# The load of w2 split into 11 rows on every partition and 8 rows on 48 partitions, in a decode kernel on one core

## Chip, cores, metric

The kernel runs on one core of a Trainium2 chip. The metric is the device time of one launch in microseconds, the median of three runs.

## The reference

A single decode step for a batch of two: a layer norm, attention of 16 query heads over a window of 2,048 positions of a cache with 8 key/value heads, and a gate from a small two-layer net.

```python
x = A_x                                   # [2, 1, 448], bf16
xn = layernorm(x)
q = xn @ wq                               # 16 heads of 256
p = softmax(q @ k[last 2048].T / 16)      # 8 kv heads, each used by two query heads
s = (p @ v[last 2048]) @ wo               # wo: [4096, 448]
h = maximum(xn @ w1, 0)                   # w1: [448, 1792]
g = silu(h @ w2)                          # w2: [1792, 448]
out = x + s * g
```

K and V of the window are 16.8 MB each, wq and wo 3.7 MB each, w1 and w2 1.6 MB each.

## The kernel before

The kernel writes its instruction lists by hand. `pr.op` and `pr.dma` append one instruction to an engine's list, with the instructions it depends on; `run` turns these into semaphores. Each engine executes its list in order, and so does SP, which issues all large loads: wq, w1, w2, the four loads of K (`d_k`, one for each unit u of 4 heads of one batch row), then V of each unit when that unit's scores are done with the buffer (`load_v`, V of unit 3 in two halves), and at the end wo in five parts of 20, 4, 5, 2 and 1 rows per partition (`WO_PARTS`). ACT issues the three small loads of x and half of the output.

The computation goes in this order. DVE and PE make the layer norm and lay it out as `xr`; PE computes q. `do_H` multiplies `xr` with w1 into the bank `qbk`, in four column groups of the PE array (`tile_position`), 448 columns in each; DVE applies the maximum (`h_n`) and transposes 32 x 32 blocks (`h_sb`), so that row 14p + j of h stands on partition p in block j. `do_F` multiplies these with w2, which is loaded the same way (partition p holds rows 14p to 14p + 13), and DVE and ACT make the gate `g_sb`.

Then DVE transposes K of each unit in place (`do_turn`, 4 instructions a unit), PE computes scores (`do_S`), DVE and ACT the softmax (`do_max`, `do_et`). After the last unit, `do_spread` and `do_pt` lay the probabilities out, `do_PV` multiplies them with V, `do_out` scales, and `do_turn_out` transposes the result into `at2`. The last product, with wo, runs in two stages: 24 rows per partition go to the bank `wbk` in four column groups, are copied to `wc` and added with 8 fp32 matmuls into `fbk`; the last 8 rows go to `fbk` directly, each matmul waiting for its part of wo. Two DVE instructions and two small stores end the kernel.

`fill(n)` issues n fp32 matmuls into a free bank whose result nobody reads. There are 7 fills: one after PV of unit 0, three in the middle of PV of unit 3, one after it, two ahead of the product with wo. PE's code is cut into bodies at marks ("block1" and so on), which are visited or hinted at ahead of their use.

Of the kernel before, what the change touches and what calls it, by code (L numbers as in the profile page):

```python
# [133 lines left out]
def bass_recurrent_scan__sliding_block_cached__dense_activation_relu__decode_kernel(  # L134
# [11 lines left out]
    B, Sq, D = A_x.shape  # L146
# [3 lines left out]
    DFF = B_w1.shape[1]  # L150
# [6 lines left out]
    NU = 4  # L157
    SLOTS = 7
    HC = HD // 2
    FC = DFF // 2  # L160
# [2 lines left out]
    PADW = 5  # L163
    WO_PARTS = [20, 4, 5, 2, 1]
    WO_TILED = 24

    es = contextlib.ExitStack()
    with es:
        pr = _Prog(nc, es)

        def named(name, shape, dt):
            return es.enter_context(nc.sbuf_tensor(name, shape, dt))
# [13 lines left out]
        wqo = named("wqo", [128, 32 * D], BF)  # L186
        assert SLOTS * HC <= 32 * D
        w1_sb = named("w1_sb", [128, SLOTS * FC], BF)
        w2_sb = named("w2_sb", [128, 14 * D], BF)
        ident = named("ident", [128, 128], BF)  # L190
        perm = named("perm", [128, 128], BF)
        par2 = named("par2", [128, 2], F32)
# [14 lines left out]
        xr = named("xr", [128, SLOTS * 4], BF)  # L207
        q_x = named("q_x", [128, 2048], BF)
        qstat = named("qstat", [128, 4 * 256], BF)
        h_n = named("h_n", [128, 448], BF)  # L210
        h_sb = named("h_sb", [128, 448], BF)
        zc = named("zc", [128, D], F32)
        wc = named("wc", [128, D], F32)
        fpad = named("fpad", [128, PADW], F32)
        ea = named("ea", [128, NCOL], F32)
        g_sb = named("g_sb", [128, NCOL], F32)
# [9 lines left out]
        half2 = named("half2", [128, 2], F32)  # L226
        rs = named("rs", [128, 2 * NU], F32)
        pt = [named(f"pt{i}", [128, 512], BF) for i in range(NU)]
        o_odd = named("o_odd", [128, DH], F32)
        at2 = named("at2", [128, 32 * PADW], BF)  # L230

# [17 lines left out]
        d_xc = [pr.dma(ACTE, x_c[32 * h:32 * h + 4, :], half(A_x, h), [p_xc]) for h in range(2)]  # L249
        wq_src = A_wq.rearrange("r (hf c) -> (r hf) c", hf=2).rearrange("(p s) c -> p (s c)", s=SLOTS)  # L250
        w1_src = B_w1.rearrange("r (hf c) -> (r hf) c", hf=2).rearrange("(p s) c -> p (s c)", s=SLOTS)
        w2_src = B_w2.rearrange("(p j) n -> p (j n)", j=14)
        wo_src = A_wo.rearrange("(p j) n -> p (j n)", j=32)

        d_k, d_v, last_S, last_PV = {}, {}, {}, {}
        st = {}
        d_wq = pr.dma(SP, wqo[:, 0:SLOTS * HC], wq_src)
        st["w1"] = pr.dma(SP, w1_sb[:, :], w1_src)
        st["w2"] = pr.dma(SP, w2_sb[:, :], w2_src)
        for u in range(NU):  # L260
            d_k[u] = pr.dma(SP, kv[u][:, :], kv_src(u, A_k_cache))

# [2 lines left out]
            out=ident[:, :], in_=ident[:, :], compare_op=ALU.not_equal, fill=1.0,  # L265
# [7 lines left out]
            out=sd[0:B, 0:1], in0=st2[0:B, 1:2], scalar1=EPS, scalar2=None, op0=ALU.add), [v_ag])  # L273
# [5 lines left out]
        def z(t):  # L279
            return a_z[t.name]  # L280
# [21 lines left out]
        for e2 in range(2):  # L302
            v_xn = pr.op(DVE, lambda e, e2=e2: e.tensor_scalar(
                out=view(xg, 128 - 127 * e2, [[256, 4], [128, 2], [2, 64]], n=B),
                in0=view(x_sb, 3 * e2, [[1, 4], [0, 2], [SLOTS, 64]], n=B),
                scalar1=st2[0:B, 0:1], scalar2=rstd[0:B, 0:1],
                op0=ALU.subtract, op1=ALU.mult), [v_rs])

        def mm(out_ap, lhsT, rhs, start, stop=False, **kw):
            return lambda e: e.matmul(out_ap, lhsT=lhsT, rhs=rhs, start=start, stop=stop,  # L310
                                      skip_group_check=True, **kw)

        for s in range(SLOTS):
# [3 lines left out]
            out=view(xr, 0, [[4, SLOTS], [2, 2], [1, 2]]), in0=view(mbk, 0, [[2, SLOTS], [0, 2], [1, 2]]),  # L317
# [3 lines left out]
        deps = [d_wq, v_xr, z(qbk)]  # L321
        for s in range(SLOTS):
            for i in range(4):
                lo = s * HC + i * 512
                m_q = pr.op(PE, mm(qbk[32 * i:32 * i + 4, :], xr[:, 4 * s:4 * s + 4], wqo[:, lo:lo + 512],
                                   s == 0, s == SLOTS - 1, tile_position=(0, 32 * i)), deps)
                deps = []
        v_q = pr.op(DVE, lambda e: e.tensor_scalar(  # L328
            out=view(q_x, 0, [[256, 8], [128, 2], [1, 32]]), in0=view(qbk, 0, [[64, 8], [1, 2], [2, 32]]),
            scalar1=SCALE, scalar2=None, op0=ALU.mult), [m_q])  # L330
        v_qx = pr.op(DVE, lambda e: e.tensor_copy(
            view(q_x, 32, [[128, 16], [32, 3], [1, 32]]), view(q_x, 0, [[128, 16], [0, 3], [1, 32]])), [v_q])
# [68 lines left out]
        def fill(n):  # L401
            for _ in range(n):
                pr.op(PE, mm(sbk[0][0:8, :], f8[:, :], kv[0][:, 0:1024].bitcast(F32), True, True),
                      [st["exp", 2], d_v[0], v_f8])

        def do_PV(u):
            bank, p, v = obk, pt[u], kv[u]
            deps = [d_v[u], st["pt", u], z(bank), st.get(("osb", u - 1))]
            for n in range(NT // 2):
                i = n % 4  # L410
                if u == NU - 1 and n == NT // 4:
                    fill(3)
                    deps = [d_vb]
                o = pr.op(PE, mm(bank[32 * i:32 * i + 16, :], p[:, 16 * n:16 * n + 16],
                                 v[:, 2 * n * DH:2 * n * DH + 2 * DH],
                                 n < 4, n >= NT // 2 - 4, tile_position=(0, 32 * i)), deps)
                deps = []
            last_PV[u] = o
# [11 lines left out]
        def do_turn_out(hg):  # L430
            deps = [st["osb", 2 + hg], v_as, st["mbk"]]
            lo = 64 * hg
            for dq in range(8):
# [4 lines left out]
            st["at"] = st["mbk"] = pr.op(DVE, lambda e: e.tensor_copy(  # L438
                view(at2, 1, [[2, B], [PADW, 32]], n=64, p0=lo), view(mbk, 288, [[32, B], [1, 32]], n=64, p0=lo)), [o, p_z])

        def do_H():
            deps = [st["w1"], v_xr, v_q]
            for s in range(SLOTS):
                for k in range(4):
                    hf, i = divmod(k, 2)
                    lo = s * FC + i * 448
                    o = pr.op(PE, mm(qbk[32 * k:32 * k + B, 0:448], xr[:, 4 * s + 2 * hf:4 * s + 2 * hf + 2],
                                     w1_sb[:, lo:lo + 448], s == 0, s == SLOTS - 1, tile_position=(0, 32 * k)), deps)
                    deps = []
            v = pr.op(DVE, lambda e: e.tensor_scalar(  # L450
                out=h_n[:, :], in0=view(qbk, 0, [[1, 14], [14, 32]]),
                scalar1=0.0, scalar2=None, op0=ALU.max), [o])
            st["h"] = pr.op(DVE, lambda e: e.transpose(h_sb[:, :], h_n[:, :]), [v])

        def do_F():
            deps = [st["w2"], st["h"], z(fbk)]
            for j in range(14):
                i = j % 4
                o = pr.op(PE, mm(fbk[32 * i:32 * i + B, 0:D], h_sb[:, 32 * j:32 * j + 2], w2_sb[:, j * D:j * D + D],
                                 j < 4, j >= 10, tile_position=(0, 32 * i)), deps)  # L460
                deps = []
            v = pr.op(DVE, lambda e: e.tensor_copy(zc[:, :], fbk[:, 0:D]), [o])
            deps = [v, v_fp, st["mbk"]]
            for c in range(4):
                k, h = divmod(c, 2)
                o = pr.op(PE, mm(mbk[32 * h:32 * h + 4, 0:NCOL], fpad[:, 1 - k:5 - k],
                                 zc[:, NCOL * c:NCOL * c + NCOL], k == 0, k == 1, tile_position=(0, 32 * h)), deps)
                deps = []
            a_e = pr.op(ACTE, lambda e: e.activation(ea[0:ROWS, :], mbk[0:ROWS, 0:NCOL], ACT.Exp, scale=-1.0), [o])
            v = pr.op(DVE, lambda e: e.tensor_scalar(  # L470
                out=ea[0:ROWS, :], in0=ea[0:ROWS, :], scalar1=1.0, scalar2=None, op0=ALU.add), [a_e])
            v = pr.op(DVE, lambda e: e.reciprocal(tmp[0:ROWS, :], ea[0:ROWS, :]), [v])
            st["g"] = st["mbk"] = pr.op(DVE, lambda e: e.tensor_tensor(
                out=g_sb[0:ROWS, :], in0=mbk[0:ROWS, 0:NCOL], in1=tmp[0:ROWS, :], op=ALU.mult), [v])
# [30 lines left out]
        for u in range(NU):  # L505
            do_PV(u)
            if u == 0:
                pr.mark("block2")
            if u in (0, NU - 1):
                fill(1)  # L510
            do_out(u)
            if u >= 2:
                do_turn_out(u - 2)
# [13 lines left out]
        v_wc = pr.op(DVE, lambda e: e.tensor_copy(wc[:, :], wbk[:, 0:D]), [o])  # L527
        pr.mark("late")
        deps = [st["g"]]

        for c in range(4):
            k, h = divmod(c, 2)
            pr.op(PE, mm(fbk[32 * h:32 * h + 4, 0:NCOL], fpad[:, 1 - k:5 - k],
                         wc[:, NCOL * c:NCOL * c + NCOL], k == 0, tile_position=(0, 32 * h)), deps + [v_wc])
        for j in range(WO_TILED, 32):
            for c in range(4):
                k, h = divmod(c, 2)
                lo = j * D + c * NCOL
                m_o = pr.op(PE, mm(fbk[32 * h:32 * h + 4, 0:NCOL], at2[:, PADW * j + 1 - k:PADW * j + 5 - k],
                                   wqo[:, lo:lo + NCOL], False, j == 31,  # L540
                                   tile_position=(0, 32 * h)), deps + [landed.get(j)])
                deps = []
# [3 lines left out]
            out=tmp[0:ROWS, :], in0=fbk[0:ROWS, 0:NCOL], in1=g_sb[0:ROWS, :], op=ALU.mult), [m_o, st["g"]])  # L546
# [35 lines left out]
```

## Time and profile before

| | |
|---|---|
| time of the launch, median of 3 | 110.18 us (110.14 to 110.25) |
| profiled execution, first to last instruction | 108.7 us |
| outside the span, by the median | about 1.5 us |
| moved from HBM | 44.11 MB, 406 GB/s over the span |
| PE busy | 58.9 us (54%), 469 matmuls |
| DVE busy | 61.5 us (57%), 84 instructions |
| ACT busy | 9.0 us (8%) |
| queue of the SP and ACT loads (q1), share of 16 engines | 95.2% |

The profile gives no launch time of its own for the profiled execution, so its span of 108.7 us is set beside the median. A core has 16 DMA engines; "DMA share" in the windows is the mean over them of the time in which a packet was under way. Queue q1 carries what SP issues and q10 what ACT issues; q8 carries instruction code. A line such as `17.99 2.78 PE L310 MATMUL qbk<-w_sb,xr ... x28` reads: from 17.99 us, for 2.78 us, 28 matmuls that write qbk. L310 is the line of a helper that all matmuls share, and L39 that of all DMA issues.

### The profile page before, as it was taken

The page shows a single profiled execution, that of the slowest core. Times are in us where ns is not written, and L with a number is a line of the kernel's source. Part 1 is how long each engine was busy: PE and PEld are TensorE (multiplying, and loading weights), DVE is VectorE, ACT ScalarE, POOL GpSimd, SP SyncE. Part 2 cuts the span into 40 slices and gives each one's busy share as a digit, 9 for nine tenths or more (in the row PEclk, how much of TensorE's full clock was granted, in tenths as well). Part 3 has the DMA queues.
Part 4 walks back from the last instruction along what each step waited for, and adds up shares of the span by engine and source line. Part 5 has one row for each costly group of instructions (what it writes and reads, how often), then busy time and mean ns, then how long its engine had stood idle before and what let it go on. Part 6 is the DMA issues. An engine that isn't in the chain of part 4 may idle for free.

```text
span 108.7 us, 1117 instructions
## 1 busy us (share of the span) xinstructions
PE 58.9 (54%) x469; PEld 15.8 (14%) x469; DVE 61.5 (57%) x84; ACT 9.0 (8%) x18; POOL 2.1 (2%) x13
## 2 busy tenths in 40 slices
PE   0001295650000069919961995299438967769672
PEld 0000023120000012101200220011023222303131
DVE  2920007634099979999999999940448332303021
ACT  2970000000000000002000200020020000000000
POOL 7000000000000000000000000000000000000000
PEclk9999999995555557995898599769965699999999
DMA  6899999989988999899989998999899899999960
GB/s 165 338 450 391 414 429 520 395 386 507 458 386 386 483 470 398 386 470 470 410 386 470 470 410 386 458 483 410 386 458 483 356 422 428 434 428 429 391 253 1
DMA packets 2487, 44.16 MB, mean 406 GB/s; under 512 B 306, under 2 KB 564, under 8 KB 820
## 3 DMA queue, kind: packets, MB, share of 16 engines
q1 hardware_dynamic: 2456, 44.11, 95.2%
q8 instruction: 3, 0.05, 0.2%
q10 hardware_dynamic: 28, 0.00, 0.0%
HBM read 44.11 MB, written 0.00 MB: 406 GB/s over the span
## 4 chain that ended last, share of the span: by engine, by line
DMA 55%; DVE 29%; PE 10%; SPq 4%; issue 1%
DMA kv<-in_A_k_cache_dram 32%; DVE kv L345 24%; DMA wqo<-in_A_wo_dram 22%; PE sbk L310 7%; SPq L39 4%; PE fbk L310 1%; PE wbk L310 1%; DVE q_x L374 1%; DVE rm L362 1%; DVE wc L527 1%; DVE rm_t L364 0%; DVE bias L368 0%; DVE bt L365 0%; DVE tmp L545 0%; DVE out_sb L547 0%
## 5 line engine op out<-in xcount | busy, mean ns | idle before, releaser
L310 PE MATMUL sbk<-kv,qstat 128*8 128x512 bf16 x128 | 30.0, 1083 | 23.0 <-DVE kv L345 23.0
L345 DVE STREAM_TRANSPOSE kv<-kv 128x2048 f32<-128x2048 f32 x16 | 35.6, 2274 | 4.6 <-DMA kv<-in_A_k_cache_dram 4.6
L310 PEld LDWEIGHTS sbk<-kv,qstat 128*8 128x8 bf16 x128 | 5.2, 107 | 46.1 <-DVE kv L345 29.0
L310 PE MATMUL obk<-kv,pt 128*16 128x512 bf16 x128 | 9.5, 441 | 2.5 <-DVE xg L426 1.2
L423 DVE TENSOR_SCALAR o_odd<-obk,rs 128x256 f32<-128x256 f32 x4 | 1.9, 484 | 11.0 <-PE obk L310 11.0
L310 PE MATMUL sbk<-kv,f 128*8 128x512 f32 x14 | 7.1, 629 | 0.0
L369 ACT ACTIVATE e_sb<-sbk,bias 128x512 bf16<-128x512 f32 x4 | 2.7, 687 | 51.8 <-DVE bias L368 51.8
L310 PE MATMUL qbk<-wqo,xr 128*4 128x512 bf16 x28 | 3.2, 626 | 4.2 <-DMA wqo<-in_A_wq_dram 4.2
L362 DVE TENSOR_REDUCE rm<-sbk 128x1 f32<-128x512 f32 x4 | 2.6, 661 | 4.8 <-PE sbk L310 4.8
L310 PE MATMUL mbk<-ident,xg 2*128 2x2 bf16 x7 | 0.3, 160 | 8.4 <-issue 8.4
L328 DVE TENSOR_SCALAR q_x<-qbk 128x512 bf16<-128x512 f32 x1 | 0.7, 692 | 7.2 <-PE qbk L310 7.2
L310 PEld LDWEIGHTS obk<-kv,pt 128*16 128x16 bf16 x128 | 3.2, 97 | 8.6 <-issue 5.0
L374 DVE STREAM_TRANSPOSE q_x<-e_sb 128x512 bf16<-128x512 bf16 x4 | 2.8, 691 | 1.7 <-ACT e_sb L369 1.7
L391 DVE TENSOR_TENSOR pt<-spk,pmask 128x512 bf16<-128x512 f32 x4 | 2.6, 683 | 0.8 <-PE spk L310 0.8
L310 PE MATMUL qbk<-w_sb,xr 128*2 128x448 bf16 x28 | 2.8, 572 | 0.0
L527 DVE COPY wc<-wbk 128x448 f32<-128x448 f32 x1 | 0.6, 625 | 3.8 <-PE wbk L310 3.8
L310 PE MATMUL spk<-q_x,perm 128*32 128x128 bf16 x16 | 0.6, 297 | 3.1 <-DVE q_x L374 3.1
L339 DVE CAST qstat<-mbk 32x256 bf16<-32x256 f32 x4 | 1.7, 420 | 0.7 <-PE mbk L310 0.7
L426 DVE SCALAR_TENSOR_TENSOR xg<-obk,rs,o_odd 128x256 bf16<-128x256 f32 x4 | 1.9, 484 | 0.1
L310 PE MATMUL wbk<-wqo,at 128*2 128x448 bf16 x24 | 1.3, 352 | 1.0 <-DMA wqo<-in_A_wo_dram 1.0
L270 DVE BATCH_NORM_STATS2 st<-x_sb 2x6 f32<-2x448 bf16 x1 | 0.6, 615 | 2.1 <-DMA x_sb<-in_A_x_dram 2.1
L310 PEld LDWEIGHTS sbk<-kv,f 128*8 128x8 f32 x14 | 1.3, 96 | 3.1 <-issue 2.6
(72 smaller groups left out, 33.0 us busy)
## 6 DMA issues: line engine op xcount, KB each, us to landing
kv<-in_A_k_cache_dram SPq DMA_DIRECT2D x4, 4096.0 KB, 39.7
kv<-in_A_v_cache_dram SPq DMA_DIRECT2D x3, 4096.0 KB, 22.1
kv<-in_A_v_cache_dram SPq DMA_DIRECT2D x2, 2048.0 KB, 17.6
wqo<-in_A_wq_dram SPq DMA_DIRECT2D x1, 3584.0 KB, 12.1
w_sb<-in_B_w_dram SPq DMA_DIRECT2D x2, 1568.0 KB, 17.0
wqo<-in_A_wo_dram SPq DMA_DIRECT2D x1, 2240.0 KB, 24.4
wqo<-in_A_wo_dram SPq DMA_DIRECT2D x1, 560.0 KB, 25.7
wqo<-in_A_wo_dram SPq DMA_DIRECT2D x1, 448.0 KB, 24.8
```

Of the source, the lines that this page charges most:

```text
L39: o = _Op(eng, lambda e: e.dma_start(dst, src), [d for d in deps if d is not None], True)
L310: return lambda e: e.matmul(out_ap, lhsT=lhsT, rhs=rhs, start=start, stop=stop, skip_group_check=True, **kw)
L328: v_q = pr.op(DVE, lambda e: e.tensor_scalar(out=view(q_x, 0, [[256, 8], [128, 2], [1, 32]]), in0=view(qbk, 0, [[64, 8], [1, 2], [2, 32]]) ...
L339: st["q"] = st["mbk"] = pr.op(DVE, lambda e, Q=Q: e.tensor_copy(qstat[32 * Q:32 * Q + 32, 256 * Q:256 * Q + 256], mbk[32 * Q:32 * Q + 32, ...
L345: st["turn", u] = pr.op(DVE, lambda e, n=n: e.transpose(kf[:, 2048 * n:2048 * n + 2048], kf[:, 2048 * n:2048 * n + 2048]), [d_k[u]])
L362: v = pr.op(DVE, lambda e: e.tensor_reduce(out=rm[:, 0:1], in_=sbk[u % 2][:, :], axis=AX.X, op=ALU.max), [last_S[u], p_z, st.get(("rmt", u ...
L369: st["exp", u] = pr.op(ACTE, lambda e: e.activation(e_sb[:, :], sbk[u % 2][:, :], ACT.Exp, bias=bias[:, 0:1], accum_out=ssum[:, u:u + 1]), ...
L374: st["et", u] = pr.op(DVE, lambda e: e.transpose(q_x[:, 512 * u:512 * u + 512], e_sb[:, :]), [st["exp", u], m_qt])
L391: st["pt", u] = pr.op(DVE, lambda e: e.tensor_tensor(out=view(pt[u], 0, [[8, 64], [2, 4], [1, 2]]), in0=view(spk, 128 * u, [[2, 64], [0, 4 ...
L423: v = pr.op(DVE, lambda e: e.tensor_scalar(out=o_odd[:, :], in0=obk[:, DH:2 * DH], scalar1=rs[:, 2 * u + 1:2 * u + 2], scalar2=None, op0=A ...
L426: st["osb", u] = pr.op(DVE, lambda e: e.scalar_tensor_tensor(out=o_sb[:, lo:lo + DH], in0=obk[:, 0:DH], scalar=rs[:, 2 * u:2 * u + 1], in1 ...
L527: v_wc = pr.op(DVE, lambda e: e.tensor_copy(wc[:, :], wbk[:, 0:D]), [o])
```

## The change

w2 is loaded in two transfers. The first takes rows 0 to 1,407, 11 to a partition. The second takes the last 384 rows, 8 to a partition, to partitions 32 to 79 of a new tile `w2_x`, which DVE zeroes before; its source is walked as twelve blocks, four rows of 7,168 bytes in each. H is cut to match: four column groups of 352 columns in `qbk`, where a group that crosses the middle of w1's columns is two matmuls, and two more matmuls per slot for the last 384 columns into `wbk`. DVE makes the maximum and the transpose for both, and F is 19 matmuls instead of 14. The tiles of h lie in the probabilities' tiles `pt`, `wc` lies in `zc`, and the copy to it also waits for the gate. One fill after PV of unit 0 and one of the three in PV of unit 3 are left out.

```diff
+    W2U = 11
+    W2X = 8
+    XA, XB = 12, 4
+    UC = 32 * W2U
+    UROWS = 128 * W2U
...
-        w2_sb = named("w2_sb", [128, 14 * D], BF)
+        w2_sb = named("w2_sb", [128, W2U * D], BF)
+        w2_x = named("w2_x", [128, W2X * D], BF)
...
-        wc = named("wc", [128, D], F32)
+        wc = zc
...
+        h_n, h_sb, h_nx, h_x = pt
...
-        w2_src = B_w2.rearrange("(p j) n -> p (j n)", j=14)
+        w2_src = B_w2[0:UROWS, :].rearrange("(p j) n -> p (j n)", j=W2U)
+        w2x_src = B_w2[UROWS:DFF, :].rearrange("(b a s) n -> a b (s n)", a=XA, b=XB)
...
         st["w2"] = pr.dma(SP, w2_sb[:, :], w2_src)
+        v_w2x = pr.op(DVE, lambda e: e.memset(w2_x[:, :].bitcast(F32), 0.0))
+        st["w2x"] = pr.dma(SP, w2_x[32:32 + XA * XB, :], w2x_src, [v_w2x])
...
                 if u == NU - 1 and n == NT // 4:
-                    fill(3)
+                    fill(2)
...
+        half_cols = FC
+        pieces = []
+        for k in range(4):
+            lo, at = UC * k, 0
+            while at < UC:
+                hf, c = divmod(lo + at, half_cols)
+                n = min(UC - at, half_cols - c)
+                pieces.append((k, hf, at, c, n))
+                at += n
+
         def do_H():
             deps = [st["w1"], v_xr, v_q]
             for s in range(SLOTS):
-                for k in range(4):
...
+                for k, hf, at, c, n in pieces:
+                    lo = s * FC + c
+                    o = pr.op(PE, mm(qbk[32 * k:32 * k + B, at:at + n], xr[:, 4 * s + 2 * hf:4 * s + 2 * hf + 2],
+                                     w1_sb[:, lo:lo + n], s == 0 and at == 0, s == SLOTS - 1,
+                                     tile_position=(0, 32 * k)), deps)
+                    deps = [z(wbk)] if s == 0 and k == 3 else []
+                for k, na in ((1, 8), (2, XA - 8)):
+                    lo = s * FC + UROWS - half_cols + (k - 1) * 8 * W2X
+                    ox = pr.op(PE, mm(view(wbk, 0, [[64, XB], [1, na * W2X]], n=B, p0=32 * k),
+                                      xr[:, 4 * s + 2:4 * s + 4], view(w1_sb, lo, [[XA * W2X, XB], [1, na * W2X]]),
+                                      s == 0, s == SLOTS - 1, tile_position=(0, 32 * k)), deps)
                     deps = []
...
         def do_F():
-            deps = [st["w2"], st["h"], z(fbk)]
-            for j in range(14):
...
+            deps = [st["w2"], st["w2x"], st["h"], z(fbk)]
+            rows = [(h_sb, w2_sb, j) for j in range(W2U)] + [(h_x, w2_x, j) for j in range(W2X)]
+            for n, (hs, ws, j) in enumerate(rows):
+                i = n % 4
+                o = pr.op(PE, mm(fbk[32 * i:32 * i + B, 0:D], hs[:, 32 * j:32 * j + 2], ws[:, j * D:j * D + D],
+                                 n < 4, n >= len(rows) - 4, tile_position=(0, 32 * i)), deps)
...
-            if u in (0, NU - 1):
+            if u == NU - 1:
                 fill(1)
...
-        v_wc = pr.op(DVE, lambda e: e.tensor_copy(wc[:, :], wbk[:, 0:D]), [o])
+        v_wc = pr.op(DVE, lambda e: e.tensor_copy(wc[:, :], wbk[:, 0:D]), [o, st["g"]])
```

More of the change, by code (lines that the diff above doesn't have):

```diff
@@ L165, in bass_recurrent_scan__sliding_block_cached__dense_activation_relu__decode_kernel @@
     WO_TILED = 24
+    W2U = 11
[3 more added lines that the diff above has]
+    UROWS = 128 * W2U
+    assert UROWS + XA * XB * W2X == DFF
     es = contextlib.ExitStack()
@@ L209, in bass_recurrent_scan__sliding_block_cached__dense_activation_relu__decode_kernel @@
         qstat = named("qstat", [128, 4 * 256], BF)
-        h_n = named("h_n", [128, 448], BF)
-        h_sb = named("h_sb", [128, 448], BF)
         zc = named("zc", [128, D], F32)
-        wc = named("wc", [128, D], F32)
+        wc = zc
         fpad = named("fpad", [128, PADW], F32)
@@ L228, in bass_recurrent_scan__sliding_block_cached__dense_activation_relu__decode_kernel @@
         pt = [named(f"pt{i}", [128, 512], BF) for i in range(NU)]
+        h_n, h_sb, h_nx, h_x = pt
+        assert UC <= 512 and 32 * W2X <= 512
         o_odd = named("o_odd", [128, DH], F32)
@@ L443, in do_H @@
             for s in range(SLOTS):
-                for k in range(4):
[L445 to L448, printed above, removed]
+                for k, hf, at, c, n in pieces:
[4 more added lines that the diff above has]
+                    deps = [z(wbk)] if s == 0 and k == 3 else []
@@ L449, in do_H @@
+                for k, na in ((1, 8), (2, XA - 8)):
[3 more added lines that the diff above has]
+                                      s == 0, s == SLOTS - 1, tile_position=(0, 32 * k)), deps)
                     deps = []
             v = pr.op(DVE, lambda e: e.tensor_scalar(
-                out=h_n[:, :], in0=view(qbk, 0, [[1, 14], [14, 32]]),
@@ L452, in do_H @@
-                scalar1=0.0, scalar2=None, op0=ALU.max), [o])
-            st["h"] = pr.op(DVE, lambda e: e.transpose(h_sb[:, :], h_n[:, :]), [v])
-        def do_F():
-            deps = [st["w2"], st["h"], z(fbk)]
-            for j in range(14):
-                i = j % 4
-                o = pr.op(PE, mm(fbk[32 * i:32 * i + B, 0:D], h_sb[:, 32 * j:32 * j + 2], w2_sb[:, j * D:j * D + D],
-                                 j < 4, j >= 10, tile_position=(0, 32 * i)), deps)
+                out=h_n[:, 0:UC], in0=view(qbk, 0, [[1, W2U], [W2U, 32]]),
@@ new lines, in do_H @@
+                scalar1=0.0, scalar2=None, op0=ALU.max), [ox])
+            vx = pr.op(DVE, lambda e: e.tensor_scalar(
+                out=h_nx[:, 0:32 * W2X], in0=view(wbk, 0, [[1, W2X], [W2X, 8], [64, XB]]),
+                scalar1=0.0, scalar2=None, op0=ALU.max), [ox])
+            st["h"] = pr.op(DVE, lambda e: e.transpose(h_sb[:, 0:UC], h_n[:, 0:UC]), [v])
+            st["h"] = pr.op(DVE, lambda e: e.transpose(h_x[:, 0:32 * W2X], h_nx[:, 0:32 * W2X]), [vx])
+        def do_F():
+            deps = [st["w2"], st["w2x"], st["h"], z(fbk)]
[4 more added lines that the diff above has]
+                                 n < 4, n >= len(rows) - 4, tile_position=(0, 32 * i)), deps)
```

## The prediction

> **What bounds the kernel now.** I read the page first, then the chain of waits, then narrow windows at the end of the span.
>
> ```profile
> DMA  6899999989988999899989998999899899999960
> ...
> DMA packets 2487, 44.16 MB, mean 406 GB/s; under 512 B 306, under 2 KB 564, under 8 KB 820
> ...
> q1 hardware_dynamic: 2456, 44.11, 95.2%
> q8 instruction: 3, 0.05, 0.2%
> q10 hardware_dynamic: 28, 0.00, 0.0%
> ...
> DMA 55%; DVE 29%; PE 10%; SPq 4%; issue 1%
> ```
>
> The DMA engines stand at 8 or 9 tenths from the second slice to the last but two. The chain's DVE 29% has to be looked at, since it could mean that loads wait for VectorE:
>
> ```profile
> 69.88 7.55 PE sbk L310 x21
> ...
> 78.67 24.36 DMA wqo<-in_A_wo_dram
> ...
> 103.16 1.38 PE wbk L310 x24
> ...
> 104.56 0.64 DVE wc L527
> ...
> 105.24 1.42 PE fbk L310 x40
> ```
>
> The first part of wo is issued at 78.67 and lands 24.36 us later. At the mean of 406 GB/s that is 9.9 MB, and V of units 2 and 3 with that part of wo (20 of 32 rows) are 10.7 MB. So when PE at last released these issues, all of V of units 2 and 3 still had to move: the chain through DVE and PE reached the queue about 10 us before the queue needed it. The kernel is one unbroken stream of 44.11 MB; its time is the end of that stream plus the PE and DVE work behind the last landings. How does the stream end?
>
> ```profile
> 104.40:104.60 0.20, 0.11 (x4) 0.00 (x0) 0.04 (x1) 0.00 (x0) 0.00 (x0) 1.00 0.99 363
> 104.60:104.80 0.20, 0.00 (x0) 0.00 (x0) 0.20 (x1) 0.00 (x0) 0.00 (x0) 1.00 0.72 256
> 104.80:105.00 0.20, 0.00 (x0) 0.00 (x0) 0.20 (x1) 0.00 (x0) 0.00 (x0) 1.00 0.45 161
> 105.00:105.20 0.20, 0.00 (x0) 0.00 (x0) 0.18 (x1) 0.00 (x0) 0.00 (x0) 1.00 0.18 63
> 105.20:105.40 0.20, 0.16 (x4) 0.16 (x6) 0.00 (x0) 0.00 (x0) 0.00 (x0) 1.00 0.14 54
> 105.40:105.60 0.20, 0.20 (x8) 0.15 (x6) 0.00 (x0) 0.00 (x0) 0.00 (x0) 1.00 0.44 131
> 105.60:105.80 0.20, 0.20 (x13) 0.20 (x10) 0.00 (x0) 0.00 (x0) 0.00 (x0) 1.00 0.12 40
> 105.80:106.00 0.20, 0.20 (x16) 0.20 (x12) 0.00 (x0) 0.00 (x0) 0.00 (x0) 1.00 0.09 31
> 106.00:106.20 0.20, 0.20 (x16) 0.19 (x12) 0.00 (x0) 0.00 (x0) 0.00 (x0) 1.00 0.02 4
> ```
>
> The last but one column is the mean share of the 16 DMA engines. It falls from 0.99 to 0.18 within 0.6 us, and 0.12 to 0.14 is left until about 106.0: two engines of 16 (2/16 = 0.125) work alone from 105.2 to 106.05. The bump at 105.4 I read as the third packet of the instruction queue (0.05 MB in three packets, 16 KB each). So 14 engines end near 105.2 and two about 0.85 us later. The two other instruction packets belong to the start of the kernel, and two engines are late; 16 KB on one engine are 0.6 us at the rate below, and all later data of that engine stands behind them. I take the lag for theirs.
>
> The landings set the last steps:
>
> ```profile
> 104.14 0.09 PEld L310 LDWEIGHTS wbk<-wqo,at 128*2 128x2 bf16 x4 [0.32 <-DMA wqo<-in_A_wo_dram]
> ```
>
> PE waits for the second part of wo until 104.14; wc, the 8 fp32 matmuls on it and the 32 on the last parts hang on that. A transfer has landed when its last engine is done, so the two late engines set each of these times.
>
> **The change part by part.** The main term is w2's split. Before, it is 128 runs of 12,544 bytes, 8 per engine: 100,352 bytes on each. After, it is 128 runs of 9,856 bytes (78,848 per engine) and 48 runs of 7,168 bytes in twelve blocks of four. How many engines a transfer uses can be counted in the queue rows. 2,456 packets on q1 are 17 transfers of 128 runs with 16 completions each, and 4 + 4 for one half of the output (17 x 144 + 8). 28 on q10 are 2 + 2 for x_sb, twice 4 + 4 for x_c and 4 + 4 for the output's other half. One completion per engine means: outer counts of 32 and 128 use 16 engines, 4 uses four, 2 uses two. Twelve blocks should then use twelve engines, with 28,672 bytes each. Twelve engines carry 107,520 bytes of w2 (+7,168), four carry 78,848 (-21,504).
>
> ```profile
> 31.70:35.11 3.41, 0.00 (x0) 0.00 (x0) 3.41 (x3) 0.00 (x0) 0.00 (x0) 0.50 1.07 461
> ```
>
> One engine moves 461 / 1.07 / 16 = 26.9 GB/s in mid stream, so this is +0.27 us on twelve engines and -0.80 us on four. If the two late ones are among the four, they end at 106.05 - 0.80 = 105.25 and the others at 105.2 + 0.27 = 105.5. Every landing of the tail then comes 0.55 us sooner (0.8 at most, if the twelve take their share at no cost). The trace does not name engines; that both late ones are among the four is where I choose, without a row to lean on.
>
> [...]
>
> What is next late, when the first part of wo lands near 102.5 instead of 103.03?
>
> ```profile
> 94.15 2.74 PE L310 MATMUL sbk<-kv,f 128*8 128x512 f32 x6
> 97.77 1.04 PE L310 MATMUL obk<-kv,pt 128*16 128x512 bf16 x16 [0.88 <-DMA kv<-in_A_v_cache_dram]
> ...
> 100.30 1.88 PE L310 MATMUL sbk<-kv,f 128*8 128x512 f32 x4
> ```
>
> The fills before it end at 102.18 now, and they hang on V's second half, which also comes sooner (97.77 to 97.2). PE is ready in time, so the end moves with the landings: -0.55.
>
> **H, F and their DVE work** lie under the stream:
>
> ```profile
> 17.99 2.78 PE L310 MATMUL qbk<-w_sb,xr 128*2 128x448 bf16 x28
> 20.82 0.62 DVE L450 TENSOR_SCALAR h_n<-qbk 128x448 bf16<-128x448 f32 x1 [1.00 <-PE qbk L310]
> 21.48 0.65 DVE L453 STREAM_TRANSPOSE h_sb<-h_n 128x448 bf16<-128x448 bf16 x1
> ...
> 22.23 0.92 PE L310 MATMUL fbk<-w_sb,h_sb 128*2 128x448 bf16 x14 [1.46 <-issue]
> ...
> 25.88 0.27 DVE L473 TENSOR_TENSOR g_sb<-mbk,tmp 36x112 f32<-36x112 f32 x1
> 29.97 8.89 DVE L345 STREAM_TRANSPOSE kv<-kv 128x2048 f32<-128x2048 f32 x4 [3.82 <-DMA kv<-in_A_k_cache_dram]
> ```
>
> H goes from 4 to 7 matmuls a slot. Its fullest column group streams 352 + 256 = 608 columns instead of 448: 2.78 x 608/448 = 3.8, so +1.0 us (+2.0 if a slot's second pieces run one behind another, 768 columns). F has 19 matmuls for 14: +0.3. DVE has two more instructions and 608 columns for 448 in (0.62 + 0.65): +0.5, and about 0.2 for their starts. g is done near 28.2 instead of 26.15, at worst 29.2. DVE's next work, the turn of K, waits for its DMA until 29.97 (29.4 after, by the same shift), so nothing waits for it. Without that cover the 10 us ahead of the V issues would take it. On the path: 0.
>
> **The zeroing of w2_x and SP's new wait.** DVE begins with a memset of 1,792 fp32 a partition, and SP issues w2's second transfer when that is done; all four K loads and everything after them on SP stand behind it.
>
> ```profile
> 1.20 2.52 SPq L39 DMA_DIRECT2D w_sb<-in_B_w_dram  x2
> ...
> 2.06 0.61 DVE L270 BATCH_NORM_STATS2 st<-x_sb 2x6 f32<-2x448 bf16 x1 [2.06 <-DMA x_sb<-in_A_x_dram]
> 12.91 3.16 PE L310 MATMUL qbk<-wqo,xr 128*4 128x512 bf16 x28 [4.17 <-DMA wqo<-in_A_wq_dram]
> L331 DVE COPY q_x<-q_x 128x1536 bf16<-128x1536 bf16 x1 | 0.6, 560 | 0.0
> L277 ACT ACTIVATE obk<-obk 128x512 uint32<-128x512 uint32 x1 | 0.5, 531 | 0.0
> ```
>
> Its price is 0.65 us by the copy (0.36 ns an element) and 1.9 us by ScalarE's zeroing (1.04 ns); I take 1.9, the row with 4-byte zeros. From about 0.75 it ends at 2.7, and SP is busy with w1 and w2 until 3.7: the wait is over when SP comes to it. The issue itself puts K back by about 0.6 us, while 6.9 MB of wq, w1 and w2 (16 us) are queued ahead. Layer norm starts 0.6 us later, and the first q matmul waits until 12.91 for wq, 4.17 us of which PE did nothing. On the path: 0. wc in zc's place adds a wait for g, done at 28, before a step at 104: 0.
>
> **Two fills fewer:**
>
> ```profile
> 85.38 1.49 PE L310 MATMUL sbk<-kv,f 128*8 128x512 f32 x2
> 86.80 1.90 PE L310 MATMUL obk<-kv,pt 128*16 128x512 bf16 x32
> ```
>
> A fill costs 0.9 us of PE's time (2.74 / 3) in a stretch where PE waits for V (0.88 at 97.77), so its removal gains nothing in the sum. What it may cost is the clock, a rival below.
>
> The sum is -0.55 us on a span of 108.7. About 1.5 us lie around the span (110.18 median), and I take them as they are: 110.18 - 0.55 = 109.6.
>
> **The rivals.** *A late engine is among the twelve.* If either is, it carries 7,168 bytes more and the whole tail comes 0.27 us later: 110.45, slower. It decides as soon as one of the two is inside. For it: nothing in the rows says where they are. [...] Chance 0.17.
>
> *The transfer is spread evenly over 16 engines after all* (48 runs, three each): w2's bytes per engine stay as they were, the late pair stays late, 110.18, no change. Against it: the four-block loads on q10. Chance 0.09.
>
> *More code.* PE gets 26 matmuls more and 2 fills less, each with a weight load; one more instruction packet may be needed, or one may come later.
>
> ```profile
> PE mbk L310 <- issue: 8.4, 1, 8.4
> ```
>
> PE's start shows what fetches can cost (8.4 us, hidden there under wq's load). In the tail nothing hides one: 0.6 us for 16 KB on an engine up to some 2 us for PE: 110.2 to 111.6. Chance 0.07.
>
> *The clock.* The granted clock is 1.00 in all the last windows above and 0.50 where PE idles (31.70). If the fills' removal halves it in the tail, the 40 last matmuls (1.42) and the last four of wbk nearly double: about +1.2, 110.8. Against it: PE's longest idle time there stays about 1 us. Chance 0.04.
>
> **How the numbers follow.** A difference of 0.2% (0.22 us) is about what a measurement of this kernel can tell from none. The forecast, 109.6, gets 0.63; its own range goes from 109.3 (the tail gains all of the 0.85) to 109.9 (the four engines' relief is felt by 0.27 only). The even spread and a little of the first rival, which lies only 0.05 us beyond the limit, are "same": 0.12. The rest is slower: 0.25. For 8 in 10 the range has to take in the even spread and the first rival, and ends at 110.5.
>
> **What would show it.** In the narrow windows, the share should fall to 0 without a plateau of 0.12, by about 105.5. The second part of wo should let PE go near 103.6, the final DMA issue should come at 106.7. q1 should count 2,456 + 48 + 12 = 2,516 packets. The plateau still there and later by 0.27 would mean the first rival; 2,520 packets the second; a fourth packet of the instruction queue the third; a granted clock of 0.50 after 97 the fourth. DVE's turn of K starting late, or gaps in the DMA row near 17 us, would prove the covers wrong.

## The result and the profile after

The changed kernel takes 112.90 us (median of 6 runs, 112.39 to 113.54), the kernel before 110.22 us (109.92 to 110.69) beside it. The ratio is 1.024, with a 95% interval of 1.021 to 1.027. It is slower by 2.7 us, where 109.6 was forecast. Here and below, runs more than 1.5% above the fastest of their kernel are left out of the ratios, but not of the medians.

The page of the changed kernel, with its engines, queues and shares of the chain:

```profile
span 111.0 us, 1165 instructions
...
PE 59.8 (54%) x491; PEld 18.4 (17%) x491; DVE 63.3 (57%) x87; ACT 9.0 (8%) x18; POOL 2.1 (2%) x13
...
q1 hardware_dynamic: 2516, 44.11, 93.1%
q8 instruction: 3, 0.05, 0.2%
...
DMA 48%; DVE 31%; PE 15%; issue 3%; SPq 1%
```

q1 carries the same bytes in the 2,516 packets that twelve engines give. The whole page also has one packet of 0.00 MB on another instruction queue, q14; none of the later kernels with a gap has it in its page. PE went from 469 matmuls to 491. "issue" in the chain, time in which an engine waited for nothing that the profile shows, rose from 1% to 3%. The last pieces of the chain of waits (start, length, what) say where:

```profile
103.10 1.17 PE wbk L320 x19
...
104.30 0.64 DVE zc L558
...
104.98 0.84 PE fbk L320 x19
105.82 2.00 issue
107.82 1.20 PE fbk L320 x21
```

Up to 104.98 the new kernel is ahead: its copy of wbk starts at 104.30 against 104.56, and its last product at 104.98 against 105.24. That is 0.26 us sooner. But the 40 matmuls (8 in fp32 on the copy, 32 on wo's last parts) that ran in one piece of 1.42 us now stop after 19. PE stands still for 2.00 us and then takes 1.20 us for the other 21. The sum is -0.26 + 2.00 + (0.84 + 1.20 - 1.42) = +2.36 us; the spans differ by 2.3 (108.7 to 111.0).

What did PE wait for? The windows of the changed kernel (length; busy time of PE, PEld, DVE, ACT, POOL; granted clock, DMA share, GB/s) show how the data end. A window counts the whole time and all bytes of a packet where the packet starts, so a packet of 1 us stands out as a bump in one window:

```profile
105.00:105.20 0.20, 0.20 (x6) 0.19 (x8) 0.00 (x0) 0.00 (x0) 0.00 (x0) 1.00 0.70 242
105.20:105.40 0.20, 0.20 (x10) 0.19 (x6) 0.00 (x0) 0.00 (x0) 0.00 (x0) 1.00 0.65 176
105.40:105.60 0.20, 0.20 (x14) 0.20 (x9) 0.00 (x0) 0.00 (x0) 0.00 (x0) 1.00 0.11 36
105.60:105.80 0.20, 0.20 (x9) 0.05 (x3) 0.00 (x0) 0.00 (x0) 0.00 (x0) 1.00 0.02 4
105.80:106.00 0.20, 0.02 (x1) 0.00 (x0) 0.00 (x0) 0.00 (x0) 0.00 (x0) 1.00 0.00 0
...
107.80:109.00 1.20, 1.18 (x21) 0.92 (x21) 0.00 (x0) 0.00 (x0) 0.00 (x0) 0.50 0.00 0
```

No packet starts between 105.8 and 109.0. The trace also records when each engine reports its share of a transfer complete. The part of wo that PE's next matmul needs was complete at 105.10, ahead of the gap, and the last part at 105.98, 1.84 us before PE goes on: data do not explain the gap. Before, fourteen engines had completed the last part by 105.52 and the late two at 106.19 and 106.34. So the transfers end 0.36 us sooner, as forecast in kind, and ten times the gain of 0.26 us on the chain is lost while PE stands still and then runs slower (2.62 us). In the last window the granted clock is 0.50, which accounts for the slow second piece.

### The profile page after: what moved, and what is told of

Its sections match the earlier page's. It is cut to its first block, busy times and chain, and to the rows that moved or that the text cites. A ratio compares the mean times of both kernels' runs of the same rounds, so it can differ in the third digit from the quotient of the medians.

```text
span 111.0 us, 1165 instructions
## 1 busy us (share of the span) xinstructions
PE 59.8 (54%) x491; PEld 18.4 (17%) x491; DVE 63.3 (57%) x87; ACT 9.0 (8%) x18; POOL 2.1 (2%) x13
## 3 DMA queue, kind: packets, MB, share of 16 engines
q1 hardware_dynamic: 2516, 44.11, 93.1%
## 4 chain that ended last, share of the span: by engine, by line
DMA 48%; DVE 31%; PE 15%; issue 3%; SPq 1%
DMA kv<-in_A_k_cache_dram 30%; DVE kv L355 24%; DMA kv<-in_A_v_cache_dram 18%; PE sbk L320 10%; PE fbk L320 2%; PE obk L320 2%; DVE w_x L268 1%; DVE q_x L384 1%; DVE rm L372 1%; PE wbk L320 1%; SPq L39 1%; DVE zc L558 1%; DVE st L280 0%; DVE rm_t L374 0%; DVE bias L378 0%
## 5 line engine op out<-in xcount | busy, mean ns | idle before, releaser
L320 PE MATMUL sbk<-kv,f 128*8 128x512 f32 x10 | 5.7, 686 | 0.0
L320 PE MATMUL qbk<-w_sb,xr 128*2 128x352 bf16 (+2 forms) x35 | 3.5, 426 | 0.0
L320 PE MATMUL wbk<-w_sb,xr 128*2 128x256 bf16 (+1 forms) x14 | 3.3, 366 | 0.0
L320 PE MATMUL fbk<-wqo,at 128*4 128x112 bf16 x32 | 1.6, 266 | 2.0 <-issue 2.0
L268 DVE MEMSET w_x<- 128x1792 f32 x1 | 1.6, 1552 | 1.2 <-PEq L598 1.2
L558 DVE COPY zc<-wbk 128x448 f32<-128x448 f32 x1 | 0.6, 625 | 2.6 <-PE wbk L320 2.6
```

The source lines that it names most:

```text
L268: v_w2x = pr.op(DVE, lambda e: e.memset(w2_x[:, :].bitcast(F32), 0.0))
```

## The experiments

Two theories for the gap. **Code:** PE has 22 matmuls more in all (26 more in H and F, around 20 us, and two fills of two records each fewer). Its instruction list is longer, and the end of the list would now lie in a further block of code (q8 moved it in packets of 16 KB, three of them). PE's last body is entered by a jump just ahead of the last product, so that block would be fetched only then. **Fills and clock:** with two fills fewer PE is left at half clock and comes out of step at the end. A third question is what the split itself is worth.

**Four small matmuls added to the kernel before, nothing else.** They are put behind H, where PE has time.

```diff
+            for _ in range(4):
+                pr.op(PE, mm(sbk[0][0:8, 0:64], ident[:, 0:8], ident[:, 0:64], True, True), [z(sbk[0])])
```

> The kernel before with 4 small matmuls more at the end of H (into a bank that is overwritten later), nothing else: w2 in one transfer, 7 fills. Code theory (PE's last instructions now lie behind the end of a 16 KB block of code that is fetched only when PE jumps into its last body): the gap of 2.0 us appears before the last one to four matmuls of fbk, although 4 matmuls are only 8 instructions; 112.2 to 112.9. Split theory (the second transfer of w2 and what it does to the landings makes the tail late) and fill theory (fewer fills, lower clock): no change, 110.2.

Measured: 111.93 us, ratio 1.017 (1.013 to 1.020). Timeline of PE at its end (start, length; in brackets the idle time before and its releaser):

```profile
105.87 0.96 PE L310 MATMUL fbk<-wqo,at 128*4 128x112 bf16 x29
108.15 0.26 PE L310 MATMUL fbk<-wqo,at 128*4 128x112 bf16 x3 [1.32 <-issue]
```

Four matmuls at 20 us open a gap from 106.83 to 108.15, with the transfers, fills and tiles of the kernel before. Three matmuls stand behind it. That points to a fixed place in the list, with room for one more matmul. Two runs test this place.

**Two, and one, of the same matmuls** (the same edit with `range(2)` and `range(1)`).

> The kernel before with 2 small matmuls more at the end of H. Code theory: with 4 more, 3 matmuls (6 instructions) stood behind the gap, so the kernel before ends about 2 instructions short of the block's end; with 2 more (4 instructions) 1 matmul stands behind a gap of about 1.3 us, and the time is that of 4 more, 111.8. A cost by the matmul: half of the 1.7 us that 4 cost, 111.0.

> The kernel before with 1 small matmul more at the end of H. Code theory: 2 instructions just fit, no gap, 110.2. A cost by the matmul: a quarter of 1.7 us, 110.6.

Measured: with two 111.75 us, ratio 1.013 (1.010 to 1.016); with one 110.16 us, ratio 0.998 (0.997 to 1.000). The timelines of PE, first with two, then with one:

```profile
106.01 1.01 PE L310 MATMUL fbk<-wqo,at 128*4 128x112 bf16 x31
108.32 0.21 PE L310 MATMUL fbk<-wqo,at 128*4 128x112 bf16 x1 [1.30 <-issue]
```

```profile
106.10 1.00 PE L310 MATMUL fbk<-wqo,at 128*4 128x112 bf16 x32
```

The second matmul costs 1.6 us, the first nothing. A step of this kind does not fit work, clock or data, of which two matmuls change hardly more than one; it fits the place of the last instructions. By this count, n additional matmuls leave n - 1 behind the gap; for the changed kernel 22 - 1 = 21, which is what its chain shows.

The windows of the kernel with two show a burst of DMA traffic that belongs to no load:

```profile
105.60:105.80 0.20, 0.18 (x4) 0.17 (x6) 0.00 (x0) 0.00 (x0) 0.00 (x0) 1.00 0.12 45
105.80:106.00 0.20, 0.20 (x8) 0.17 (x6) 0.00 (x0) 0.00 (x0) 0.00 (x0) 1.00 0.43 131
106.00:106.20 0.20, 0.20 (x12) 0.20 (x10) 0.00 (x0) 0.00 (x0) 0.00 (x0) 1.00 0.09 31
```

The same view of the kernel with four has it one window earlier:

```profile
105.60:105.80 0.20, 0.20 (x8) 0.17 (x6) 0.00 (x0) 0.00 (x0) 0.00 (x0) 1.00 0.43 136
```

Above the two late engines the burst moves (131 - 45) GB/s x 0.2 us = 17 KB, one packet of the instruction queue (0.05 MB in 3). The trace's packet records have it: with two matmuls it starts at 105.94 and takes 0.95 us, with four at 105.78 and as long. PE goes on at 108.32 and 108.15, 1.43 us after its end in each. In the changed kernel the packet runs from 105.22 to 106.37 and PE goes on at 107.82, 1.45 us later; the two other kernels with a gap, below, have 1.37 and 1.38. The kernel before has the packet at 105.54 too, and shows no gap behind it.

**The fills put back into the changed kernel.**

```diff
-                    fill(2)
+                    fill(3)
...
-            if u == NU - 1:
+            if u in (0, NU - 1):
                 fill(1)
```

> The changed kernel with the two fills back (7 as before). Fill theory: the clock stays at 1.0 to the end, no gap, 109.7 to 110.2. Code theory: 8 instructions more, so the gap stays at 2.0 us and stands 4 matmuls earlier (25 instead of 21 matmuls of fbk behind it); 112.4 to 112.9. Split theory: as it was, 112.4 to 112.9.

Measured: 113.17 us, ratio 1.028 (1.024 to 1.032).

```profile
105.07 0.36 PE L320 MATMUL fbk<-wqo,at 128*4 128x112 bf16 x7
107.62 1.07 PE L320 MATMUL fbk<-wqo,at 128*4 128x112 bf16 x25 [2.19 <-issue]
```

The theory of fills falls: with all seven the gap is still there, 2.19 us in which the granted clock is 1.00, and in the changed kernel it is 1.00 there too. The gap has also moved. A fill is two matmul records (PE has 495 here, 26 more than before), and 26 - 1 = 25 stand behind the gap. So leaving two fills out had, if anything, shortened the gap; the times of the two kernels do not differ clearly.

**The split without the code for it.** The two transfers, the memset and the shared tiles in the kernel before, with H and F as they were; three of F's blocks read `w2_x`.

```diff
         st["w2"] = pr.dma(SP, w2_sb[:, :], w2_src)
+        v_w2x = pr.op(DVE, lambda e: e.memset(w2_x[:, :].bitcast(F32), 0.0))
+        st["w2x"] = pr.dma(SP, w2_x[32:80, :], w2x_src, [v_w2x])
...
+                ws, jj = (w2_sb, j) if j < 11 else (w2_x, j - 11)
```

> The kernel before with w2's two transfers, the zeroing of w2_x and the shared tiles, but H and F with the instructions of before: F takes 11 blocks from w2_sb and 3 from w2_x, so the product with w2 is not the reference's. 7 fills. Code theory: PE has not one instruction more, so no gap, and the split shows its own effect: landings 0.3 to 0.5 us earlier, 109.7 to 109.9. Split theory: the loss is here, 112 to 113. Fill theory: no loss, 109.7 to 110.2.

Measured: 110.01 us, ratio 0.997 (0.994 to 1.000). No gap, and one engine is left at work where two were late:

```profile
105.40:105.60 0.20, 0.20 (x12) 0.20 (x10) 0.00 (x0) 0.00 (x0) 0.00 (x0) 1.00 0.07 22
105.60:105.80 0.20, 0.20 (x16) 0.20 (x11) 0.00 (x0) 0.00 (x0) 0.00 (x0) 1.00 0.05 18
105.80:106.00 0.20, 0.20 (x16) 0.20 (x10) 0.00 (x0) 0.00 (x0) 0.00 (x0) 1.00 0.30 82
```

One engine of 16 is 0.06. It works alone until 105.8 (the burst after it is again the code packet). The split gains 0.3%, hardly more than can be measured; the 0.55 us of the forecast (0.5%) lie just inside the interval. The completions show who ends last. For w2's first transfer the pair reports at 19.52 and 19.73 and the latest of the others at 18.91. For w2_x the last of the twelve reports at 20.00, 1.09 us after that 18.91, so the pair is not among the twelve but among the four that are spared. The engine that ends last now, at 106.12, 0.36 us behind the next, was by its lag the third latest already when wq landed (12.23, where the pair had 12.87 and 13.08).

**The changed kernel without the added code.** The 14 matmuls of H into `wbk` and the 8 of F on `w2_x` are left out, all else stays, the five fills too.

```diff
-                for k, na in ((1, 8), (2, XA - 8)):
+                for k, na in ():
...
-            rows = [(h_sb, w2_sb, j) for j in range(W2U)] + [(h_x, w2_x, j) for j in range(W2X)]
+            rows = [(h_sb, w2_sb, j) for j in range(W2U)] + []
```

> The changed kernel without the 14 matmuls of H into wbk and the 8 matmuls of F on w2_x (the last 384 of the 1,792 hidden rows are left out of the product); its transfers, the zeroing, DVE's instructions, the shared tiles and the 5 fills stay. 22 matmuls are 44 instructions, and 42 stood behind the gap. Code theory: no gap, and what is left is the split's gain: 109.7 to 110.0. If the loss came from anything else that is still in it (fewer fills, the second transfer, shared tiles, the zeroing): 112.4 to 112.9.

Measured: 110.49 us, ratio 1.001 (0.998 to 1.004). The gap is gone; the PV of unit 3 is not wholly back at its pace (16 matmuls in 1.26 us, 1.04 before and 1.88 in the changed kernel):

```profile
97.77 1.26 PE L320 MATMUL obk<-kv,pt 128*16 128x512 bf16 x16 [2.09 <-DMA kv<-in_A_v_cache_dram]
...
105.66 1.00 PE L320 MATMUL fbk<-wqo,at 128*4 128x112 bf16 x32
```

The 2.3% between this ratio and that of the changed kernel go with the 22 matmuls. The windows of this run:

```profile
105.60:105.80 0.20, 0.20 (x12) 0.20 (x8) 0.00 (x0) 0.00 (x0) 0.00 (x0) 1.00 0.06 22
105.80:106.00 0.20, 0.20 (x16) 0.20 (x11) 0.00 (x0) 0.00 (x0) 0.00 (x0) 1.00 0.06 22
```

One engine again is at work alone, here until 106.0. The gain of 0.2 to 0.5 us that I expected of the split did not show here; together with the run above, the split is worth between nothing and about 0.3%. The engine that ends last here, at 106.36, was again, by its lag, the third latest from wq on (12.47; in the profile of the kernel before the third latest had 11.84).

**An earlier jump.** If the block is fetched while PE still has to wait for wo, the gap should close. The mark of the last body moves ahead of the product into `wbk`.

```diff
         fill(2)
+        pr.mark("late")
         deps = [st["at"], z(wbk)]
...
-        pr.mark("late")
```

> The changed kernel with the jump into PE's last body moved ahead of the 24 matmuls with wo (the mark 'late' stands right after the last fills); the same matmuls in the same order. Code theory: the packet is fetched while PE waits for wo, the gap of 2.0 us and the low clock behind it go, 109.7 to 110.1. Split theory and fill theory: the jump has nothing to do with it, 112.4 to 112.9.

Measured: 111.04 us, ratio 1.007 (1.002 to 1.011). No gap; PE now waits for wo:

```profile
104.78 0.56 PE L320 MATMUL fbk<-zc,fpad 128*4 128x112 f32 x8 [0.73 <-DVE zc L559]
...
106.03 1.12 PE L320 MATMUL fbk<-wqo,at 128*4 128x112 bf16 x32 [0.69 <-DMA wqo<-in_A_wo_dram]
```

```profile
105.60:105.80 0.20, 0.00 (x0) 0.00 (x0) 0.00 (x0) 0.00 (x0) 0.00 (x0) 1.00 0.07 27
105.80:106.00 0.20, 0.00 (x0) 0.00 (x0) 0.00 (x0) 0.00 (x0) 0.00 (x0) 1.00 0.07 27
106.00:106.20 0.20, 0.17 (x8) 0.17 (x10) 0.00 (x0) 0.00 (x0) 0.00 (x0) 1.00 0.05 18
106.20:106.40 0.20, 0.20 (x16) 0.20 (x12) 0.00 (x0) 0.00 (x0) 0.00 (x0) 1.00 0.05 18
```

By the ratios nearly three quarters of the loss are back. In this run one engine works alone until 106.4, later than in any run of the split so far, and the queue of the code has 4 packets for 3. One of them now starts inside the stream, at 103.56, and takes 0.89 us. The completions show what it does: for the second part of wo the last two engines report at 103.59 and 103.65, side by side; for the third, fifteen report by 105.04 and one at 105.99, and that lag stays to the last part (105.86 and 106.84). So in this run the packet held up the data of its engine by 0.95 us, about its own length. The runs scatter in two groups (110.2 to 110.6, among them the one profiled, and 111.5 to 111.7), and why is open.

**The same jump in the kernel before, and in the changed kernel with all fills.** The first asks what the packet in the stream costs without the split, the second whether the fills cause the scatter.

> The kernel before with the jump into PE's last body ahead of the 24 matmuls with wo, as in the changed kernel with the early jump. There is no gap to remove. If a code packet that is fetched inside the stream makes its DMA engine, and so the last landing, later by 0.6 to 1.0 us: 110.8 to 111.2. If the 0.8 us that the early jump still lost came from the changed kernel's other parts: 110.2.

> The changed kernel with the early jump and with the two fills back. With the early jump alone the time was 111.04, with single times from 110.2 to 111.7. If the slower of these come from PE's clock (5 fills leave it at half speed in the last matmuls), 7 fills bring 110.2 to 110.5 throughout. If they come from the code packet, fetched inside the stream on an engine that then ends last, the fills change nothing: 111.0, spread as before.

Measured: in the kernel before 110.39 us, ratio 1.001 (0.999 to 1.002), near the 110.2 expected if the packet costs nothing there, and not 110.8 to 111.2; in the changed kernel with seven fills 110.75 us, ratio 1.004 (1.000 to 1.007), scattered from 109.86 to 111.33 as without them. So neither the jump alone nor the fills explain what is left. With seven fills, too, one engine falls 0.9 us behind in wo's third part, at 106.15 against 105.22. In the kernel before the share at the end is

```profile
105.60:105.80 0.20, 0.20 (x8) 0.17 (x4) 0.00 (x0) 0.00 (x0) 0.00 (x0) 1.00 0.22 58
105.80:106.00 0.20, 0.20 (x12) 0.20 (x8) 0.00 (x0) 0.00 (x0) 0.00 (x0) 1.00 0.15 49
106.00:106.20 0.20, 0.20 (x16) 0.20 (x12) 0.00 (x0) 0.00 (x0) 0.00 (x0) 1.00 0.09 31
```

0.22 is about three engines where there were two (0.12), and they end when the pair ends. The completions confirm it: after the code packet at 104.24 a third engine reports with the pair (106.39, 106.51 and 106.57 for the last part, the other thirteen by 105.78). The lag of the pair gave it room, and the split takes this room away.

**The block fetched early.** The changed kernel, with a jump at PE's start to the end of its code and back, as it is done already for other bodies.

```diff
-            eng.br_eq(zero, 0, "part0", "part3").branch_hint(told_visit)
+            eng.br("visit4")
...
+        with body("visit4"):
+            eng.br_eq(zero, 0, "part0", "done").branch_hint(told_visit)
+        with body("done"):
+            emit(eng, ops[-1:], seen)
```

> The changed kernel, and PE's start-up jumps once more, to a body at the end of its code, before it begins (its first matmul comes later than 8.5 us). Code theory: the last block of code is fetched at the start, the gap of 2.0 us goes; the packet (0.6 us on one engine) is paid while wq loads, and makes the tail later by 0 (on an engine with slack) to 0.6 us: 109.9 to 110.5. If PE keeps no block that it fetched so early, or the gap is no fetch: 112.4 to 112.9 or more.

Measured: 113.13 us, ratio 1.025 (1.022 to 1.028), no gain; the gap is 2.23 us before the last 20 matmuls, and the queue of the code counts 5 packets. By the packet records the visit brings no third packet at the start: there are two, at 2.01 and 5.46, as in the changed kernel (1.91 and 5.81). The others start at 65.20, at 106.88, ahead of the gap, and at 110.28, after the last matmul. So the visit did not bring the block early in a way that the trace shows, and the run does not tell whether a block fetched at the start would still be there 100 us later.

**The relief without new code.** In the kernel before, w2 in its old place: six rows on all partitions, then the other eight on partitions 0 to 31, on 80 to 127, and on 32 to 79 in four transfers of twelve partitions.

```diff
-        st["w2"] = pr.dma(SP, w2_sb[:, :], w2_src)
+        st["w2"] = [pr.dma(SP, w2_sb[:, 0:W2C], w2_src[:, 0:W2C]),
+                    pr.dma(SP, w2_sb[0:32, W2C:], w2_src[0:32, W2C:]),
+                    pr.dma(SP, w2_sb[80:128, W2C:], w2_src[80:128, W2C:])]
+        for i in range(4):
+            st["w2"].append(pr.dma(SP, w2_sb[32 + i:80:4, W2C:], w2_src[32 + i:80:4, W2C:]))
```

> The kernel before, with w2 in its old place but moved by seven transfers: 6 rows on all partitions, 8 rows on partitions 0 to 31 and on 80 to 127, and 8 rows on 32 to 79 in four transfers of twelve partitions; H, F and fills as before, the whole product computed. The same bytes are taken off four DMA engines as in the change, without one PE instruction more. Code theory: as the split alone, 0.3% less than before, 109.7 to 110.0 (up to 110.4 if the shorter runs of 2,688 and 3,584 bytes cost more). If the split's small gain came from the tiles or waits that the other kernel shared: 110.2.

Measured: 113.41 us, ratio 1.030 (1.027 to 1.032), 3.0 us above the highest time expected. There is no gap; the whole tail is later. Windows of this kernel while w2 is loaded:

```profile
16.00:20.00 4.00, 2.51 (x52) 1.04 (x44) 2.69 (x6) 0.00 (x0) 0.00 (x0) 1.00 1.08 253
20.00:24.00 4.00, 0.00 (x0) 0.00 (x0) 0.87 (x2) 0.00 (x0) 0.00 (x0) 0.94 1.06 365
```

and of the kernel before:

```profile
16.00:20.00 4.00, 2.60 (x44) 1.29 (x44) 2.93 (x6) 0.00 (x0) 0.00 (x0) 1.00 1.15 495
20.00:24.00 4.00, 1.82 (x30) 0.44 (x20) 1.89 (x3) 0.00 (x0) 0.00 (x0) 1.00 0.99 426
```

The engines' share is much the same (1.08 for 1.15, 1.06 for 0.99), but they move 253 GB/s for 495 and 365 for 426. Over 8 us that is 1.2 MB, 3.0 us at 406 GB/s, and the spans differ by 3.2 (108.7 to 111.9). Which property of these narrow transfers slows them, their few partitions or their steps, was not taken apart.

## Why the prediction was wrong

**The step that failed** is "More code". I gave it a chance of 0.07 and times of 110.2 to 111.6, and put PE's added instructions into the sum at nothing, because H and F run under the stream. That cover is real for the time of these matmuls and means nothing for their room: what they push back is the end of the list. I had the number that mattered, 26 matmuls more and two fills (four records) less, and did not ask how much room was left at the end of the list. It had room for one (one more matmul: 110.16 us, two: 111.75). Also the price of some 2 us at most was short, and no row or run had given it: 2.00 us of gap and 0.62 us of slower matmuls around it, 2.7 us in the medians. PE's 8.4 us at the start are no measure of it: its first matmul needs `xg`, which DVE finished at 6.16, and the second code packet ended at 6.69. The sign that I named was wrong as well: the code's queue has no fourth packet (3 on q8, as before). A code packet came at the end before too (105.54), with no gap behind it; that PE now needs its code is my reading of the step at the second added matmul.

What was late is not the target of the jump, behind which PE ran 15 to 39 matmuls without a stop, but something further on in its list. That it is the next block of code is an inference: the code packets are of 16 KB, and the stop comes with the second added matmul and not with the first, but no trace names what a packet holds. So soon behind a jump, the gap measured 1.30 to 2.23 us in five kernels.

**The main term** was right in its mechanism, and its prices came out: by the completions the third latest engine takes 17.15 us from wq's landing to that of the first K before, and the last of the twelve takes 17.43 with the split, 0.28 us more (0.27 forecast); and in the changed kernel none of w2_x's twelve is late (the last reports at 19.84; a late one would at about 20.7). So both late engines are among the four, and the plateau of 0.12 went. The even spread falls with the 2,516 packets. That choice I made without a row, and it was in part luck: it held in six of the seven traces with the split, but with the visit to the end one of the late two was among the twelve (20.41, the next 19.91).

What I left out is that the engines' lags differ from launch to launch: the third latest at wq's landing is anywhere from 11.84 to 12.47 in these traces, and it ends last once the pair is relieved. The last landing of wo is at 105.80 to 106.36 in four traces with the split, without an extra code packet, and at 106.34 to 106.80 in four with w2 in one transfer: 0.54 us sooner on average, with a spread as large. The comparisons of times show less, 0 to 0.3%; why they do is open. In the kernel before the pair is 0.9 to 1.0 us late already when wq lands (12.73 and 12.87, the others by 11.84), after code packets at 1.90 and 5.73. That fits the cause that I took, but no run took those packets away.

**H, F, the memset and SP's wait** were hidden, as said. The timeline of the changed kernel holds them, and in its last two lines what the paragraph on the clock needs:

```profile
1.18 1.55 DVE L268 MEMSET w_x<- 128x1792 f32 x1 [1.18 <-PEq L598]
...
4.99 3.45 SPq L39 DMA_DIRECT2D kv<-in_A_k_cache_dram  x4
...
27.64 0.27 DVE L504 TENSOR_TENSOR g_sb<-mbk,tmp 36x112 f32<-36x112 f32 x1
29.53 2.31 DVE L355 STREAM_TRANSPOSE kv<-kv 128x2048 f32<-128x2048 f32 x1 [1.62 <-DMA kv<-in_A_k_cache_dram]
...
97.35 1.88 PE L320 MATMUL obk<-kv,pt 128*16 128x512 bf16 x16 [2.10 <-DMA kv<-in_A_v_cache_dram]
...
103.79 0.09 PEld L320 LDWEIGHTS wbk<-wqo,at 128*2 128x2 bf16 x4 [0.20 <-DMA wqo<-in_A_wo_dram]
```

The memset took 1.55 us, between the bounds of 0.65 and 1.9. K is issued at 4.99 instead of 3.77, 1.2 us later and not 0.6, ahead of K's turn in the stream, since the second part of w2 is moving until 19.84. g is done at 27.91 (28.2 forecast), and DVE still waits 1.62 us for K, of 3.82 us before: the cover held, with less left than it had.

**The clock** did what the fourth rival feared, in another place and for little. With one fill less PE waits 2.10 us for V instead of 0.88 and then runs at half clock: 1.88 us at a granted clock of 0.51 for what took 1.04 at 1.00. It is back in time, since it still waits for the second part of wo at 103.79 (103.6 forecast, 104.14 before). At the end the half clock came with the gap and added its 0.62 us there.

## What to carry to other kernels

An added instruction can have two prices, its time and its room: of two small matmuls added at 20 us the first cost nothing here and the second 1.6 us, by a stop behind a jump near the end. So look at how far an addition pushes back the end of the list of the engine that ends the kernel. When a transfer is cut so as to relieve the engines that end last, the gain reaches only to the next of them (0 to 0.3% here, where 0.5% was forecast), so look at each engine's last completion and not at the mean of the rest, in more than one execution. And when the gap is closed by an earlier fetch, the fetch moves into the stream: it cost nothing in the kernel before (ratio 1.001), where its engine did not end after the late pair, and held up the last landing in the changed kernel (106.84, the other engines by 105.86), where it did.

## What the hardware showed that was not expected

In all five kernels with a gap PE went on 1.37 to 1.45 us after the end of the last code packet ahead of it; the packet itself took 0.93 to 1.32 us, and started 0.9 to 1.0 us after PE's last product into `wbk` (1.5 us with the visit to the end). In the changed kernel the three add up to 3.55 us, from the end of that product at 104.27 to 107.82. Meanwhile PE still runs 19 matmuls there, and 39 with two added, and the gap is 2.00 and 1.30 us. In the changed kernel a code packet inside the load stream put the data of its engine back by 0.9 to 1.0 us. A lag that an engine has when the first load lands stays with it nearly whole: in the kernel before the pair is 0.9 and 1.0 us behind the rest for wq and 0.7 and 0.8 us for the last part of wo. And seven transfers of the same bytes of w2, four of them on twelve partitions each, went with 253 GB/s instead of 495 in the core's stream, at nearly the same DMA share.
